# Sums of the last 64 queries on 64x64 tiles, with partial sums in two PSUM banks, and six output buffers

## The chip, the cores and the metric

The kernel runs on one core of one Trainium2 chip. The metric is the device time of one execution in microseconds. The kernel before takes 341.7 us (median of 3 runs, 341.29 to 341.9). TensorE was granted 0.995 to 1.0 of its clock in all runs but those of one experiment, which is marked. A ratio is the mean time of one kernel's fast runs over that of the other's of the same rounds, so it is not quite the ratio of the medians quoted beside it.

## The reference

Attention over 8 batches, 12 heads, 448 positions of 64 dimensions, with one added to the softmax denominator (in its shifted form), followed by a feed-forward layer with a maximum over three products (put together from the reference's two functions):

```python
scores = scale * np.matmul(q, k.transpose(0, 1, 3, 2))
e = np.exp(scores - m)
attn = e / (np.sum(e, axis=-1, keepdims=True) + np.exp(-m) + 1e-09)
x = np.matmul(attn, v)          # then heads side by side: 3584 x 768
h = np.maximum(np.maximum(x @ w1, x @ w2), x @ w3)
out = h @ w_out
```

## The kernel before

The heads are worked in 24 groups of four, two pairs of heads each (`i` is the group, `pr` the pair). Each group takes three visits. In a visit TensorE computes scores of one group, then, in two visits of three, for one pair of the group before the weighted sum over keys (`av`), then pieces of the feed-forward layer that keep it busy. 448 queries are four blocks of 128 columns, of which the last is only half needed. 448 keys are three chunks of 128 and a tail of 64; the tails of both heads share 128 partitions and are summed on 64x64 tiles:

```python
def av_tail(i, ej, pr, ws=(0, 1, 2, 3)):         # (cut)
    for j, w in enumerate(ws):
        for hh in range(2):
            for half in range(2):
                nc.tensor.matmul(out=ps[half * HP : half * HP + HP, hh, j * D1 : (j + 1) * D1], ...)  # 64x64

def av_main(i, ej, pr, ws=(0, 1, 2, 3)):         # (cut)
    for hh in range(2):
        for j, w in enumerate(ws):
            for c, x in enumerate((X1, X3, X2)):
                nc.tensor.matmul(out=ps[:, hh, j * D1 : (j + 1) * D1], lhsT=eF[:, o : o + 128], ...)  # 128x128
    nc.vector.tensor_scalar(out=rb[:, :, 0:nw], in0=acc[:, :, :, D], ... op0=ALU.add)
    nc.vector.reciprocal(out=rb[:, :, 0:nw], in_=rb[:, :, 0:nw])
    nc.vector.tensor_tensor(out=xn[i][...], in0=acc[:, :, :, 0:D], in1=rb..., op=ALU.mult)
```

Column `D` of each sum is the softmax denominator, since the values carry a column of constants. A piece of the feed-forward layer is a group of six matmuls into one of two PSUM buffers, evacuated by VectorE:

```python
ps_b = ctx.enter_context(tc.tile_pool(name="ps_b", bufs=2, space=bass.MemoryType.PSUM))
def up_piece(b, fcs, i, q0, qn):                  # (cut)
    p_i = ps_b.tile([128, 512], FP32, tag="b", name="p_i")
    ...six matmuls...
    if i == 0: nc.vector.tensor_copy(out=dst, in_=src)
    else:      nc.vector.tensor_tensor(out=dst, in0=dst, in1=src, op=ALU.max)
```

`out_piece` does the same for the last product (`op_ps`, evacuated into `o_sb`, then a transfer to `out`).

The softmax here doesn't subtract the row's maximum and nothing guards it: scores larger than these inputs give would overflow.

## Time and profile before

| | kernel before |
|---|---|
| time, median | 341.7 us |
| TensorE (PE) busy | 330.3 us, 97% |
| VectorE (DVE) busy | 188.4 us, 55% |
| chain that ended last | PE 93%, DVE 2% |
| idle of PE just before p_i groups | 1.1 us |

The busy share says who has no room. The chain, followed back from the last instruction, says whose work the end waited for. The timeline says what happens around one sum. The lines are in the prediction.

### The profile page before, as it was taken

Reading aid. Unit: us, or ns where it says so; the run is one execution under the profiler, and the core shown is the slowest. Engines: PE = TensorE matmul, PEld = TensorE weight load, DVE = VectorE, ACT = ScalarE, POOL = GpSimd, SP = SyncE. Lnnn points to the kernel's source line nnn. Section 1 sums busy time; section 2 is a strip of 40 time slices with the busy share of each in tenths; the row PEclk is TensorE's granted clock in tenths of the full one; section 3 lists DMA queues with packets and bytes.
Section 4 is the critical chain, followed back from the end, with each engine's and each line's share of the span. In section 5 each row is a group of like instructions: output and inputs, shape, how many; then the busy total and the mean of one; then the engine's idle time right before and its main releaser. Section 6 shows DMA issues by size and latency. Waiting matters only on the chain.

```text
span 340.8 us, 9819 instructions
## 1 busy us (share of the span) xinstructions
PE 330.3 (97%) x4174; PEld 199.6 (59%) x4174; DVE 188.4 (55%) x410; ACT 151.2 (44%) x181; POOL 146.7 (43%) x260
## 2 busy tenths in 40 slices
PE   7899999999999999999999999999999999999994
PEld 4668787855555645555655655565545655565552
DVE  4556675565545365546456556556556556465552
ACT  3858855654554535463544454463544454200000
POOL 8596578971937072925267070946252000000000
PEclk9999999999999999999999999999999999999999
DMA  8999999699996999999986999999960440133006
GB/s 145 190 191 206 203 205 197 115 170 212 134 164 60 178 213 110 156 138 185 157 119 90 190 199 116 155 127 194 167 115 10 119 123 3 31 78 95 0 19 167
DMA packets 84813, 46.42 MB, mean 136 GB/s; under 512 B 53281, under 2 KB 81313, under 8 KB 84769
## 3 DMA queue, kind: packets, MB, share of 16 engines
q0 software_dynamic: 29120, 21.80, 48.6%
q1 hardware_dynamic: 55264, 23.60, 36.7%
q8 instruction: 32, 0.52, 0.6%
q10 hardware_dynamic: 384, 0.39, 0.4%
q14 instruction: 13, 0.10, 0.1%
HBM read 44.04 MB, written 11.01 MB: 162 GB/s over the span
## 4 chain that ended last, share of the span: by engine, by line
PE 93%; ACT 2%; DVE 2%; issue 1%; ACTq 0%
PE p_i L440 48%; PE op_ps L464 16%; PE avp L357 12%; PE stp L300 12%; PE avp L340 2%; ACT e L320 2%; PE warm L171 1%; PE trT L225 1%; ACT QT L184 1%; DVE QT L186 1%; PE trT L209 1%; DVE xn L373 1%; PE xtp L413 0%; PE xtp L400 0%; DVE xT L406 0%
## 5 line engine op out<-in xcount | busy, mean ns | idle before, releaser
L320 ACT ACTIVATE e<-stp 128x896 f16<-128x896 f32 (+4 forms) x171 | 144.3, 905 | 138.2 <-PE stp L300 138.0
L440 PE MATMUL p_i<-xT,w 128*128 128x448 f16 (+2 forms) x972 | 173.4, 332 | 1.1 <-DVE o_sb L471 0.8
L440 PEld LDWEIGHTS <-w 128*128 128x128 f16 x972 | 90.0, 98 | 69.0 <-issue 6.6
L245 POOL COPY QT<-QT 64x384 f16<-64x384 f16 (+1 forms) x84 | 46.9, 559 | 95.4 <-DMA QT<-ld_q 65.0
L451 DVE TENSOR_TENSOR hT<-hT,p_i 128x448 f16<-128x448 f16 (+2 forms) x96 | 59.7, 621 | 43.0 <-PE p_i L440 42.8
L464 PE MATMUL op_ps<-w,hT 128*128 128x384 f16 (+2 forms) x342 | 58.1, 323 | 0.0
L300 PE MATMUL stp<-QT,KT 64*64 64x448 f16 (+2 forms) x756 | 48.4, 339 | 2.3 <-ACT e L320 0.9
L464 PEld LDWEIGHTS <-hT 128*128 128x128 f16 x342 | 32.1, 98 | 23.0 <-issue 2.0
L471 DVE TENSOR_SCALAR o_sb<-op_ps 128x384 f32<-128x384 f32 (+2 forms) x57 | 31.2, 549 | 25.8 <-PE op_ps L464 22.7
L357 PE MATMUL avp<-vx,e 128*128 128x65 f16 x1152 | 45.4, 193 | 0.0
L449 DVE CAST hT<-p_i 128x448 f16<-128x448 f32 (+2 forms) x48 | 30.0, 625 | 24.3 <-PE p_i L440 24.2
L357 PEld LDWEIGHTS <-e 128*128 128x128 f16 x1152 | 38.8, 97 | 2.3
L373 DVE TENSOR_TENSOR xn<-avp,rb 128x512 f16<-128x512 f32 (+1 forms) x54 | 34.1, 632 | 1.9
L300 PEld LDWEIGHTS <-KT 64*64 64x64 f16 x756 | 16.0, 105 | 27.0 <-issue 24.2
L367 DVE TENSOR_SCALAR rb<-avp 128x8 f32<-128x8 f32 (+1 forms) x54 | 8.9, 165 | 39.4 <-PE avp L357 39.2
L383 POOL COPY vx<-ld_v 128x768 f16<-128x768 f16 x21 | 17.2, 820 | 8.3 <-issue 4.7
L340 PEld LDWEIGHTS <-e 64*64 64x64 f16 x768 | 14.7, 107 | 8.0 <-issue 1.2
L102 POOL DMA_DIRECT2D ld_q<-in_q_dram x24 | 17.2, 718 | 2.1 <-DMA w<-in_moe_w_dram 1.1
L102 POOL DMA_DIRECT2D ld_k<-in_k_dram x24 | 17.2, 718 | 1.9 <-DMA w<-in_moe_w_out_dram 1.0
L115 POOL DMA_DIRECT2D ld_v<-in_v_dram x24 | 15.1, 631 | 2.6 <-DMA w<-in_moe_w_dram 1.4
L340 PE MATMUL avp<-vt,e 64*64 64x65 f16 x768 | 15.4, 192 | 0.5 <-ACT e L320 0.4
L112 POOL DMA_DIRECT2D ld_v<-in_v_dram x24 | 15.2, 633 | 1.2 <-DMA w<-in_moe_w_dram 1.2
(43 smaller groups left out, 88.2 us busy)
## 6 DMA issues: line engine op xcount, KB each, us to landing
out_dram<-o_sb SPq DMA_DIRECT2D x54, 192.0 KB, 3.2
ld_v<-in_v_dram POOLq DMA_DIRECT2D x48, 128.0 KB, 4.8
ld_k<-in_k_dram POOLq DMA_DIRECT2D x23, 224.0 KB, 6.2
ld_q<-in_q_dram POOLq DMA_DIRECT2D x23, 224.0 KB, 7.0
w<-in_moe_w_dram POOLq DMA_DIRECT2D x9, 384.0 KB, 9.5
w<-in_moe_w_out_dram POOLq DMA_DIRECT2D x3, 384.0 KB, 8.5
xT<-xn SPq DMA_TRANSPOSE x18, 4.3
QT<-ld_q SPq DMA_TRANSPOSE x17, 5.1
```

What stands on the lines that cost most here:

```text
L102: nc.gpsimd.dma_start(out=tiles[nm][:, 1 : NP * T + 1].rearrange("x (r t) d -> x r (t d)", r=NP)[:, p0:p1], in_=src[:, p0:p1],)
L245: eng.tensor_copy(out=t[d0 : d0 + HP, o * 128 : (o + n) * 128], in_=t[s0 : s0 + HP, a * 128 : (a + n) * 128],)
L300: nc.tensor.matmul(out=stp[half * HP : half * HP + HP, par, j * qn : (j + 1) * qn], lhsT=k_block(i, pr, h2, x[half]), rhs=q_cols(i, pr, h2 ...
L320: nc.scalar.activation(out=dst, in_=src, func=AF.Exp, scale=scale)
L340: nc.tensor.matmul(out=ps[half * HP : half * HP + HP, hh, j * D1 : (j + 1) * D1], lhsT=eF[hh * HP : hh * HP + HP, o : o + HP], rhs=vt[hh * ...
L357: nc.tensor.matmul(out=ps[:, hh, j * D1 : (j + 1) * D1], lhsT=eF[:, o : o + 128], rhs=vx[:, 2 * pr + hh, (x[0]), 0:D1], start=False, stop= ...
L373: nc.vector.tensor_tensor(out=xn[i][:, pr, ws[0] : ws[0] + nw].rearrange("p j h d -> p h j d"), in0=acc[:, :, :, 0:D], in1=rb[:, :, 0:nw]. ...
L440: nc.tensor.matmul(out=p_i[:, j * qn : (j + 1) * qn], lhsT=w_sb[i][:, dc, ts(fc, 128)], rhs=xT[b][:, dc, q0 : q0 + qn], start=(dc == 0), s ...
L449: nc.vector.tensor_copy(out=dst, in_=src)
L451: nc.vector.tensor_tensor(out=dst, in0=dst, in1=src, op=ALU.max)
L464: nc.tensor.matmul(out=op_ps[:, 0:w], lhsT=hT[bp][:, fc, ts(t, 128)], rhs=wout_sb[:, fc, c : c + w], start=(fc == 0), stop=(fc == NFC - 1),)
L471: nc.vector.tensor_scalar(out=o_sb[:, c : c + w], in0=op_ps[:, 0:w], scalar1=1.0 / LAMBDA, scalar2=None, op0=ALU.mult,)
```

## The change

The last 64 queries of each pair had their sums on full 128x128 matmuls of which half the output columns were thrown away. The change computes them as 64x64 tiles, in sets of four (the 64x64 tail tiles of the kernel before start mostly 3 to 4 ns apart within a set, and the sets 29 to 36 ns apart in nearly all sums): rows of the array are the two halves of the keys, columns the two heads. In the code, two tiles that hold different key halves write two different PSUM banks, so the halves are added on VectorE. It applies from group 6 on, in 36 sums. Two smaller parts come along: the opening is reordered without two dummy matmuls, and the output gets six buffers. The results `xn` move into three fixed buffers, whose part that nothing writes is cleared once (cut below).

```diff
-    out_pool = ctx.enter_context(tc.tile_pool(name="outp", bufs=3))
+    out_pool = ctx.enter_context(tc.tile_pool(name="outp", bufs=6))
+    def av_last(i, ej, pr):                      # (cut) 2 tail tiles and 12 tiles of 64x64
+        for c, x in enumerate((X1, X3, X2)):
+            for r in range(2):
+                for hh in range(2):
+                    tile_mm(r, hh, o, rhs, c == 2)   # out=ps[head hh's half, bank r]
     # av_main, after the denominators of the three full blocks
+        if last:
+            nc.vector.tensor_copy(out=end, in_=ps[:, 1, 3 * D1 : 4 * D1])
+            nc.vector.tensor_tensor(out=end, in0=ps[:, 0, 3 * D1 : 4 * D1], in1=end, op=ALU.add)
+            nc.vector.tensor_scalar(out=rb_all[:, 2 * nw :], in0=end[:, D:], ... op0=ALU.add)
     nc.vector.reciprocal(...); nc.vector.tensor_tensor(... op=ALU.mult)   # now 3 blocks
+        if last:
+            for hh in range(2):                  # head 1 moves from partitions 64.. to 0..
+                nc.vector.tensor_scalar(out=xn[i][0:HP, pr, 3, hh], in0=end[h, 0:D],
+                                        scalar1=rb_all[h, 2 * nw :], op0=ALU.mult)
-    warm(2)
-    attend("O", 2, ("v", 1, 0), ("v", 1, 1), ("v", 2, 0))
+    attend("O", 2, ("v", 1, 0))
     attend("E", 0, S01)
+    attend("O", 2, ("v", 1, 1), ("v", 2, 0), ("v", 2, 1))
```

More of the change, by code (lines that the diff above doesn't have):

```diff
@@ L58 @@
     PE_X = 2
+    LAST = 6
     NEB = 2
@@ L64 @@
     small = ctx.enter_context(tc.tile_pool(name="small", bufs=3))
-    xn_pool = ctx.enter_context(tc.tile_pool(name="xn", bufs=3))
     xt_pool = ctx.enter_context(tc.tile_pool(name="xt", bufs=3))
     ht_pool = ctx.enter_context(tc.tile_pool(name="ht", bufs=2))
-    out_pool = ctx.enter_context(tc.tile_pool(name="outp", bufs=3))
+    out_pool = ctx.enter_context(tc.tile_pool(name="outp", bufs=6))
     ps_s = ctx.enter_context(tc.tile_pool(name="ps_s", bufs=3, space=bass.MemoryType.PSUM))
@@ L166 @@
         nc.vector.memset(blk[:, :, NO : NO + HP], 0.0)
+    xn_buf = [cpool.tile([P, NP, 4, 2, D], MMDT, name=f"xn{j}") for j in range(NV)]
+    for j in range(NV):
+        nc.vector.memset(xn_buf[j][HP:P, :, 3], 0.0)
     def warm(n, cols=512):
@@ L347, in av_tail, with tile_mm, av_main @@
                     )
-    def av_main(i, ej, pr, ws=(0, 1, 2, 3)):
+    def av_last(i, ej, pr):
+        eF, vx, vt = e_buf[ej], v_buf[i % NV], vt_buf[i % NV]
+        ps = avs[i, pr]
+        def tile_mm(r, hh, o, rhs, stop):
+            nc.tensor.matmul(
+                out=ps[hh * HP : hh * HP + HP, r, 3 * D1 : 4 * D1],
+                lhsT=eF[r * HP : r * HP + HP, o : o + HP],
+                rhs=rhs,
+                start=False,
+                stop=stop,
+                skip_group_check=True,
+            )
+        n = where[pr, None, TL]
+        for hh in range(2):
+            tile_mm(hh, hh, e_col(n, 3), vt[hh * HP : hh * HP + HP, pr, 0:D1], False)
+        for c, x in enumerate((X1, X3, X2)):
+            for r in range(2):
+                for hh in range(2):
+                    o = e_col(where[pr, hh, x], 3)
+                    rhs = vx[r * HP : r * HP + HP, 2 * pr + hh, x[0], 0:D1]
+                    tile_mm(r, hh, o, rhs, c == 2)
+    def av_main(i, ej, pr, ws=(0, 1, 2, 3), last=False):
         eF, vx = e_buf[ej], v_buf[i % NV]
@@ L365, in av_main @@
         acc = ps[:, :, 0 : nw * D1].rearrange("p h (j d) -> p h j d", d=D1)
-        rb = small.tile([P, 2, 4], FP32, tag="rb", name="rb")
+        rb_all = small.tile([P, 2 * nw + 1], FP32, tag=f"rb{nw}", name="rb")
+        rb = rb_all[:, 0 : 2 * nw].rearrange("p (h j) -> p h j", h=2)
         nc.vector.tensor_scalar(
-            out=rb[:, :, 0:nw], in0=acc[:, :, :, D], scalar1=1.0 / LAMBDA, scalar2=None, op0=ALU.add
+            out=rb, in0=acc[:, :, :, D], scalar1=1.0 / LAMBDA, scalar2=None, op0=ALU.add
         )
-        nc.vector.reciprocal(out=rb[:, :, 0:nw], in_=rb[:, :, 0:nw])
+        if last:
+            end = small.tile([P, D1], FP32, tag="end", name="end")
+            nc.vector.tensor_copy(out=end, in_=ps[:, 1, 3 * D1 : 4 * D1])
+            nc.vector.tensor_tensor(
+                out=end, in0=ps[:, 0, 3 * D1 : 4 * D1], in1=end, op=ALU.add
+            )
+            nc.vector.tensor_scalar(
+                out=rb_all[:, 2 * nw :], in0=end[:, D:], scalar1=1.0 / LAMBDA, scalar2=None,
+                op0=ALU.add,
+            )
+        rb_in = rb_all if last else rb_all[:, 0 : 2 * nw]
+        nc.vector.reciprocal(out=rb_in, in_=rb_in)
         if i not in xn:
-            xn[i] = xn_pool.tile([P, NP, 4, 2, D], MMDT, tag="xn", name="xn")
+            xn[i] = xn_buf[i % NV]
         nc.vector.tensor_tensor(
@@ L375, in av_main @@
             in0=acc[:, :, :, 0:D],
-            in1=rb[:, :, 0:nw].unsqueeze(3).to_broadcast([P, 2, nw, D]),
+            in1=rb.unsqueeze(3).to_broadcast([P, 2, nw, D]),
             op=ALU.mult,
         )
+        if last:
+            for hh in range(2):
+                h = slice(hh * HP, hh * HP + HP)
+                nc.vector.tensor_scalar(
+                    out=xn[i][0:HP, pr, 3, hh], in0=end[h, 0:D], scalar1=rb_all[h, 2 * nw :],
+                    scalar2=None, op0=ALU.mult,
+                )
     def prep_v(i, eng):
@@ L528, in av @@
     def av(i, ej, pr, part):
-        av_tail(i, ej, pr, PW[part])
-        av_main(i, ej, pr, PW[part])
+        if i >= LAST:
+            av_tail(i, ej, pr, (0, 1, 2))
+            av_last(i, ej, pr)
+            av_main(i, ej, pr, (0, 1, 2), True)
+        else:
+            av_tail(i, ej, pr, PW[part])
+            av_main(i, ej, pr, PW[part])
     load_weight(0)
@@ L568 @@
     x_transpose_pe(0, "O")
-    warm(2)
-    attend("O", 2, ("v", 1, 0), ("v", 1, 1), ("v", 2, 0))
+    attend("O", 2, ("v", 1, 0))
     attend("E", 0, S01)
+    attend("O", 2, ("v", 1, 1), ("v", 2, 0), ("v", 2, 1))
     x_transpose_pe(1, "O")
-    attend("E", 0, ("v", 2, 1), S23)
+    attend("E", 0, S23)
     x_transpose_pe(2, "O")
```

## The prediction

> **What bounds the kernel now.** I read the page first: the busy shares, then the chain that ended last.
>
> ```profile
> PE 330.3 (97%) x4174; PEld 199.6 (59%) x4174; DVE 188.4 (55%) x410; ACT 151.2 (44%) x181; POOL 146.7 (43%) x260
> PE 93%; ACT 2%; DVE 2%; issue 1%; ACTq 0%
> ```
>
> TensorE is busy for 330.3 of 340.8 us and carries 93% of the chain, at full granted clock. So a nanosecond taken from TensorE is a nanosecond of the span, and so is one for which TensorE is made to wait. VectorE is busy 55% of the time, which looks like ample room. Whether it is depends on when VectorE's work falls, so next I read the timeline around one sum (one pair of heads, one `av` call).
>
> ```profile
> 183.12 0.29 PE L340 MATMUL avp<-vt,e 64*64 64x65 f16 x16
> 183.35 0.92 PE L357 MATMUL avp<-vx,e 128*128 128x65 f16 x24
> ...
> 184.12 1.29 PE L440 MATMUL p_i<-xT,w 128*128 128x448 f16 x6
> 184.31 0.17 DVE L367 TENSOR_SCALAR rb<-avp 128x8 f32<-128x8 f32 x1 [0.86 <-PE avp L357]
> 184.51 0.20 DVE L370 RECIPROCAL rb<-rb 128x8 f32<-128x8 f32 x1
> 184.75 0.69 DVE L373 TENSOR_TENSOR xn<-avp,rb 128x512 f16<-128x512 f32 x1
> 185.45 0.62 DVE L451 TENSOR_TENSOR hT<-hT,p_i 128x448 f16<-128x448 f16 x1
> ```
>
> The sum takes 16 matmuls on 64x64 tiles (the key tails), then 24 full ones; TensorE goes straight on to the next group of the feed-forward part (p_i, six matmuls, 1.135 us from group to group). VectorE begins to normalise 0.19 us after that group's start, needs three instructions that end 1.13 us later, and is then just in time to evacuate the first group. The groups rotate through two PSUM buffers, so the third group after a sum can't start before the first is evacuated. That makes VectorE's 1.13 us a quantity with a limit.
>
> The same view elsewhere shows the limit being hit once, by another cause:
>
> ```profile
> 119.11 1.02 DVE L471 TENSOR_SCALAR o_sb<-op_ps 128x384 f32<-128x384 f32 x2 [2.92 <-PE avp L357]
> 119.72 0.54 PE L440 MATMUL p_i<-xT,w 128*128 128x448 f16 x2 [0.76 <-DVE o_sb L471]
> ```
>
> VectorE stood for 2.92 us. The releaser named had ended earlier; the instruction order shows that this eviction also waits for the output transfers that free one of three output buffers. TensorE restarted 0.05 us after the first eviction ended (119.11 + 0.555 = 119.67), having lost 0.76 us. So a late eviction does stop TensorE.
>
> [...] single records have the last four tail matmuls at 183.217 us and the first full one at 183.349, 132 ns against some 31 within a mode. The change puts its small matmuls between tails and full ones, so it adds no switch. [...] (3 to 4 ns within a set of four; the next four follow 29 to 33 ns later). [...] a copy from partition 64 started 0.03 us after the previous copy's end, where unheld independent instructions start some 0.08 us before it.
>
> **The change on TensorE.** It applies from group 6 on: 18 groups by 2 pairs, 36 sums. Each loses six full matmuls of 31.8 ns ((184.117 - 183.353) / 24): -191 ns. In place of tail matmuls in four sets of four there are three sets of tails, and for the last queries four more rounds on the busiest tiles: seven rounds for four, at 31 ns: +93 ns. Net about -97 ns, times 36 = **-3.5 us**. Six output buffers remove the one stall: **-0.8 us**. At the start, the two dummy matmuls go and the first scores of group 0's other queries come earlier; the sum there then waits for ScalarE instead, so of the 0.43 us little is won, but the waits of 0.37 us for xn and some 0.4 us for xT near 22.7 and 23.4 us shrink in part: **-0.3 us**, an estimate. Together -4.6 us.
>
> **The change on VectorE.** These rows size the new instructions (groups by line, shapes apart; the last two numbers before the bar's idle time are busy us and mean ns):
>
> ```profile
> L449 DVE CAST hT<-p_i 128x448 f16<-128x448 f32 x42 | 26.2, 625 | 20.6 <-PE p_i L440 20.6
> L373 DVE TENSOR_TENSOR xn<-avp,rb 128x512 f16<-128x512 f32 x42 | 29.0, 692 | 1.4
> L373 DVE TENSOR_TENSOR xn<-avp,rb 128x256 f16<-128x256 f32 x12 | 5.1, 425 | 0.4
> L370 DVE RECIPROCAL rb<-rb 128x8 f32<-128x8 f32 x42 | 8.5, 203 | 1.4
> L370 DVE RECIPROCAL rb<-rb 128x4 f32<-128x4 f32 x12 | 2.1, 179 | 0.4
> L186 DVE CAST ld_k<-first_k 128x448 f16<-128x448 f32 x1 | 0.4, 396 | 2.0 <-DMA first_k<-in_k_dram 2.0
> ```
>
> From L373, (692 - 425) / 256 = 1.04 ns an element and 158 ns fixed from PSUM. [...] Hence: sums' column of 6: 164 ns (167 for 8, 161 for 4); copy of 128x65: 226; add of 128x65: 226; the 128x1 addition: about 150; reciprocal of 7: 197; product of 128x384: 558; two products of 64x64: about 190 each (least certain). Dependent instructions follow after 34 ns, independent ones overlap by 80 ns. Laid out from the first one's start: 0; copy 0.084 to 0.310; add 0.344 to 0.570; addition 0.604 to 0.754; reciprocal 0.788 to 0.985; product 1.02 to 1.58; first small product 1.50 to 1.69; second, held, 1.72 to 1.91. The next eviction starts at 1.83 if it reads only PSUM, or 1.94 if it also reads hT [...]. Today it could start at 1.05. So the sequence grows by some 0.8 us; 36 of these are about 28 us of VectorE time, which by itself would cost nothing.
>
> **What the longer sequence costs.** Count from the first group's start after a sum. For p_i groups the third can start at 2.27 us. Its buffer is free at 0.19 + 1.83 (or 1.94) + 0.62 of eviction + 0.05 = 2.69 (2.80): a stall of 0.42 or 0.53. For op_ps groups (0.975 us each, eviction 0.556): 0.19 + 1.83 + 0.556 + 0.05 = 2.63 against 1.95: 0.67. If only two groups follow before the next scores, the pause of scores and sums hides it.
> From the TensorE timeline I counted what follows each of the 36 sums: 14 times three p_i groups (first eviction a cast 7 times, a maximum 7 times), 5 times three op_ps groups, once a p_i and two op_ps groups; the last two sums are back to back; 14 are followed by two groups only. Stalls: 14 x 0.475 = 6.65; 5 x 0.67 = 3.35; 2.80 - 2.11 = 0.69; and for the last pair, whose sequences queue on VectorE, 1.35. Sum **+12.0 us**. Today the same sum gives no stall (0.19 + 1.14 + 0.62 + 0.05 = 2.00 < 2.27), and the page agrees: all idle of TensorE before p_i groups is 1.1 us.
>
> Result: 341.7 - 4.6 + 12.0 = **349 us**, +2.1%.
>
> **Rivals.** (a) The stalls don't come, because VectorE's small instructions take nearer 60 to 100 ns than 150 to 190: the next eviction starts near 1.55, the stalls shrink to some 5.5 us and the total is about 342.5. For it speaks that VectorE is idle 45%, and memsets take as little as 62 ns; against it, that every record reading data takes at least 151 ns. (b) Stalls are short or absent and the TensorE saving shows in full: 337 us. Against it speaks the two-buffer count above. (c) The small matmuls don't overlap as the tails do, say because each waits for its weights: then the saving is nearly nil, and the total 352. Against it speaks the measured 31 ns a round, weight loads included. (d) POOL's copies in SBUF slow VectorE's new SBUF instructions: copies of 64x128 vary from 168 to some 276 ns today; 0.1 us more a sum adds 2 us.
>
> **Range and chances.** Each 0.1 us in VectorE's sequence moves 21 stalls, so 2.1 us. I take 0.15 us either way for that, and 1.5 us for TensorE's part: 344 to 353. The middle lies just above the 2% line (348.5), so slower and within are nearly even; faster by 2% needs both no stall and a larger saving than TensorE has: 0.02.
>
> **What would show it.** Right: TensorE idle before p_i and op_ps groups, waiting for VectorE, grows from 1.1 to some 12 us, in pieces of 0.4 to 0.7 us at the third group after a sum; full sum matmuls go from 1152 to 936; the wait of 2.92 us is gone. Wrong: that idle stays below 4 us, or the next eviction follows the first normalising instruction by under 1.5 us, or the small matmuls take more than 31 ns for four.

The sum keeps all its terms: 341.7 - 4.6 + 12.0 = 349.1, given as 349. The 190 ns of the two products stand as estimate alone: they came from the 396 ns of the one ld_k record and a rate from SBUF that no run shows. The eviction at 1.83 or 1.94 us, and so the +12.0 us, hang on them. The 0.11 us between these two starts are put together from the copies from partition 64 (three records, which started 31 to 32 ns after the end of the copy before) and the 80 ns by which independent instructions overlap; that a maximum would be held like those copies was an estimate too (after the change a cast starts at 1.91 and a maximum at 2.02 us). The numbers in brackets, 3 to 4 ns and 29 to 33, are of the starts of the tail matmuls.

## The result, and the profile after

The changed kernel takes **357.84 us** (357.08 to 358.18, 4 runs) against 341.54 us: ratio 1.0473, 95% interval 1.0453 to 1.0494. It is slower by 16.3 us, more than twice the 7.3 us that were predicted, and outside the range of 344 to 353 us. The page of the changed kernel, its busy shares and its chain:

```profile
PE 330.4 (93%) x4316; PEld 196.4 (55%) x4316; DVE 218.9 (62%) x593; ACT 151.0 (43%) x181; POOL 146.5 (41%) x260
PE 73%; DVE 20%; issue 3%; ACT 2%; ACTq 0%; DVEq 0%
```

VectorE's part of the chain went from 2% to 20%, though it is busy only 62% of the time. TensorE's busy time did not fall although its work did. That is an effect of the record: a p_i matmul is shown for about 350 ns where the next one normally starts after 189, so each stop adds some 0.16 us of shown busy time.

The timeline around one sum that op_ps groups follow (start in us, duration in us, engine, line, operation, count, idle time before it and what ended it):

```profile
198.26 2.11 PE L514 MATMUL op_ps<-w,hT 128*128 128x384 f16 x12
198.46 0.17 DVE L399 TENSOR_SCALAR rb<-avp 128x6 f32<-128x6 f32 x1 [0.83 <-PE avp L388]
198.54 0.21 DVE L404 COPY end<-avp 128x65 f32<-128x65 f32 x1
198.79 0.23 DVE L405 TENSOR_TENSOR end<-avp,end 128x65 f32<-128x65 f32 x1
199.05 0.15 DVE L408 TENSOR_SCALAR rb<-end 128x1 f32<-128x1 f32 x1
199.24 0.20 DVE L413 RECIPROCAL rb<-rb 128x7 f32<-128x7 f32 x1
...
199.47 0.56 DVE L416 TENSOR_TENSOR xn<-avp,rb 128x384 f16<-128x384 f32 x1
199.95 0.51 DVE L425 TENSOR_SCALAR xn<-end,rb 64x64 f16<-64x64 f32 x2
200.37 1.02 DVE L521 TENSOR_SCALAR o_sb<-op_ps 128x384 f32<-128x384 f32 x2
...
200.98 1.14 PE L514 MATMUL op_ps<-w,hT 128*128 128x384 f16 x6 [0.60 <-DVE o_sb L521]
```

Two groups (12 matmuls) fill the two buffers. The third stands still until VectorE has worked through eight instructions and evacuated the first. The eviction starts 1.91 us after the first normalising instruction (1.05 before).

Where POOL copies in SBUF at the same time, it is worse. Here the two products take 1.16 us together, and TensorE stands for 1.12:

```profile
184.54 2.38 POOL L249 COPY QT<-QT 64x384 f16<-64x384 f16 x4 [2.59 <-DMA QT<-ld_q]
184.60 1.16 DVE L425 TENSOR_SCALAR xn<-end,rb 64x64 f16<-64x64 f32 x2
...
185.79 0.62 DVE L501 TENSOR_TENSOR hT<-hT,p_i 128x448 f16<-128x448 f16 x1
...
186.46 1.29 PE L490 MATMUL p_i<-xT,w 128*128 128x448 f16 x6 [1.12 <-DVE hT L501]
```

And one kind of stop comes already in the second group. The op_ps group needs hT, which the eviction of the p_i group before it writes; its sixth matmul waits for that:

```profile
190.12 0.98 PE L514 MATMUL op_ps<-w,hT 128*128 128x384 f16 x5
...
191.32 0.62 DVE L501 TENSOR_TENSOR hT<-hT,p_i 128x448 f16<-128x448 f16 x1
...
192.00 0.34 PE L514 MATMUL op_ps<-w,hT 128*128 128x384 f16 x1 [0.90 <-DVE hT L501]
```

The groups by line, shapes apart (busy us, mean ns after the bar), give the sizes of VectorE's new instructions:

```profile
L425 DVE TENSOR_SCALAR xn<-end,rb 64x64 f16<-64x64 f32 x72 | 22.2, 308 | 0.5
L416 DVE TENSOR_TENSOR xn<-avp,rb 128x384 f16<-128x384 f32 x36 | 20.1, 557 | 1.4 <-DVE rb L413 0.2
L405 DVE TENSOR_TENSOR end<-avp,end 128x65 f32<-128x65 f32 x36 | 8.2, 227 | 1.2
L404 DVE COPY end<-avp 128x65 f32<-128x65 f32 x36 | 7.8, 217 | 0.0
L413 DVE RECIPROCAL rb<-rb 128x7 f32<-128x7 f32 x36 | 7.2, 201 | 1.2
L399 DVE TENSOR_SCALAR rb<-avp 128x6 f32<-128x6 f32 x36 | 5.9, 164 | 23.8 <-PE avp L388 23.8
L408 DVE TENSOR_SCALAR rb<-end 128x1 f32<-128x1 f32 x36 | 5.5, 154 | 1.2
```

All are within 9 ns of the prediction but the products, of mean 308 ns instead of 190. Instruction by instruction, where no POOL record overlaps them, the first takes 237 and the second 252 ns; the longest take 527 and 654.

I added up how much later than its normal pitch each feed-forward matmul starts after the 36 sums. Before: 0.3 us. After: **18.4 us**, behind 23 sums. The loss is smaller because TensorE saves some 4 us elsewhere; 1 to 2 us of the loss are not in these delays (below).

### The profile page after: what moved, and what is told of

Same layout as the page of the kernel before. It is cut to its first block, busy times and chain, and to the rows that moved or that the text cites. A ratio compares the mean times of both kernels' runs of the same rounds, so it can differ in the third digit from the quotient of the medians.

```text
span 355.3 us, 10283 instructions
## 1 busy us (share of the span) xinstructions
PE 330.4 (93%) x4316; PEld 196.4 (55%) x4316; DVE 218.9 (62%) x593; ACT 151.0 (43%) x181; POOL 146.5 (41%) x260
## 4 chain that ended last, share of the span: by engine, by line
PE 73%; DVE 20%; issue 3%; ACT 2%; ACTq 0%; DVEq 0%
PE p_i L490 35%; PE op_ps L514 13%; PE stp L304 11%; PE avp L388 9%; DVE xn L425 4%; DVE xn L416 4%; DVE hT L501 2%; DVE rb L413 2%; ACT e L324 2%; DVE end L405 2%; PE avp L344 1%; DVE rb L399 1%; PE warm L175 1%; PE avp L361 1%; DVE rb L408 1%
## 5 line engine op out<-in xcount | busy, mean ns | idle before, releaser
L490 PE MATMUL p_i<-xT,w 128*128 128x448 f16 (+2 forms) x972 | 175.6, 332 | 7.7 <-DVE hT L501 4.2
L514 PE MATMUL op_ps<-w,hT 128*128 128x384 f16 (+2 forms) x342 | 59.1, 323 | 7.5 <-DVE hT L501 4.3
L388 PE MATMUL avp<-vx,e 128*128 128x65 f16 x936 | 38.6, 194 | 0.0
L388 PEld LDWEIGHTS <-e 128*128 128x128 f16 x936 | 32.0, 97 | 2.3
L416 DVE TENSOR_TENSOR xn<-avp,rb 128x384 f16<-128x384 f32 (+2 forms) x54 | 29.3, 543 | 2.1 <-DVE rb L413 0.2
L399 DVE TENSOR_SCALAR rb<-avp 128x6 f32<-128x6 f32 (+2 forms) x54 | 8.8, 164 | 33.5 <-PE avp L388 33.5
L425 DVE TENSOR_SCALAR xn<-end,rb 64x64 f16<-64x64 f32 x72 | 22.2, 308 | 0.5
L344 PEld LDWEIGHTS <-e 64*64 64x64 f16 x624 | 13.7, 107 | 7.9 <-issue 1.4
```

The source lines that it names most:

```text
L416: nc.vector.tensor_tensor(out=xn[i][:, pr, ws[0] : ws[0] + nw].rearrange("p j h d -> p h j d"), in0=acc[:, :, :, 0:D], in1=rb.unsqueeze(3) ...
L425: nc.vector.tensor_scalar(out=xn[i][0:HP, pr, 3, hh], in0=end[h, 0:D], scalar1=rb_all[h, 2 * nw :], scalar2=None, op0=ALU.mult,)
L490: nc.tensor.matmul(out=p_i[:, j * qn : (j + 1) * qn], lhsT=w_sb[i][:, dc, ts(fc, 128)], rhs=xT[b][:, dc, q0 : q0 + qn], start=(dc == 0), s ...
L514: nc.tensor.matmul(out=op_ps[:, 0:w], lhsT=hT[bp][:, fc, ts(t, 128)], rhs=wout_sb[:, fc, c : c + w], start=(fc == 0), stop=(fc == NFC - 1),)
```

## The experiments

The theory: the loss is made by the length of VectorE's sequence between a sum and the first eviction behind it. Rivals: TensorE's small matmuls cost time themselves; one of the two side parts does harm; POOL's copies lengthen the new instructions; the amount of VectorE work counts and not its place.

**One part at a time.** Four kernels, all starting from the kernel before. The first takes only the opening:

```diff
-    warm(2)
-    attend("O", 2, ("v", 1, 0), ("v", 1, 1), ("v", 2, 0))
+    attend("O", 2, ("v", 1, 0))
     attend("E", 0, S01)
+    attend("O", 2, ("v", 1, 1), ("v", 2, 0), ("v", 2, 1))
```

> The kernel before with only the new order of the opening (no two dummy matmuls, first scores of group 0's other queries earlier). If the loss comes from VectorE's longer sequence after each sum: about 341.3 us, 0.2 us below the kernel before. Rival, the new opening upsets the later rhythm: well above 345 us.

Measured: 341.12 against 341.85 us, ratio 0.9979 (0.9966 to 0.9993). A gain of 0.7 us, no harm.

The second takes only the output buffers:

```diff
-    out_pool = ctx.enter_context(tc.tile_pool(name="outp", bufs=3))
+    out_pool = ctx.enter_context(tc.tile_pool(name="outp", bufs=6))
```

> The kernel before with only six output buffers. Expected: the 2.92 us wait of VectorE and the 0.76 us stop of TensorE go, 340.8 us. Rival, the stop is only moved elsewhere: 341.5 us, unchanged. In either case no loss.

Measured: 341.49 against 341.85 us, ratio 0.9989 (0.9976 to 1.0002). The wait and the stop are gone from the trace. The gain, 0.4 us, is not clear of noise; no harm either.

The third takes only TensorE's side of the new sums:

```diff
+            av_tail(i, ej, pr, (0, 1, 2)); av_last(i, ej, pr); av_main(i, ej, pr, (0, 1, 2), True)
     # av_main: no copy, addition, inverse or products for the last 64 queries (left zero, wrong on purpose)
```

> The kernel before with the 64x64 matmuls for the last 64 queries, but none of the new VectorE instructions (those results are left out, so the output is wrong on purpose). If TensorE's new matmuls save what the count of rounds says: 36 times 0.1 us, 338.0 us, with no new stalls of TensorE. Rival, the small matmuls or the larger number of instructions cost TensorE time themselves: 345 us or more.

Measured: 338.8 against 341.85 us, ratio 0.9913 (0.9899 to 0.9927). The small matmuls save 3.0 us. Its page:

```profile
PE 326.3 (97%) x4318; PEld 195.6 (58%) x4318; DVE 183.9 (55%) x413; ACT 151.0 (45%) x181; POOL 146.6 (44%) x260
```

TensorE's busy time falls by 4 us here, where no stops hide the saving. The first rival falls.

The fourth takes only VectorE's side, with the full matmuls kept:

```diff
+            nc.vector.tensor_copy(out=end, in_=ps[:, 1, 3 * D1 : 4 * D1])
+            nc.vector.tensor_tensor(out=end, in0=ps[:, 0, 3 * D1 : 4 * D1], in1=end, op=ALU.add)
+            nc.vector.tensor_scalar(out=r1, in0=end[:, D:], ... op0=ALU.add)
         nc.vector.reciprocal(...); nc.vector.tensor_tensor(...)      # as before
+            for hh in range(2): nc.vector.tensor_scalar(out=scr[:, hh], in0=end[h, 0:D], scalar1=r1[h], ...)
```

> The kernel before with its matmuls unchanged, plus five VectorE instructions of the changed kernel's kinds and shapes in each of the 36 sums (results to a scratch tile; the output stays right). If the longer sequence alone makes the loss: stalls of 18 us as in the changed kernel, and some 2.5 us more because the large product keeps its 128x512 (0.134 us in each of about 21 stalls): about 361 us. Rival, the loss needs the new matmuls: about 342 us.

Measured: 361.06 against 341.85 us, ratio 1.0563 (1.0548 to 1.0577), with correct output. Its page, busy shares and chain:

```profile
PE 333.6 (93%) x4174; PEld 199.6 (56%) x4174; DVE 221.9 (62%) x590; ACT 151.1 (42%) x181; POOL 146.9 (41%) x260
PE 70%; DVE 20%; issue 3%; DMA 3%; ACT 2%; POOL 1%; POOLq 0%; ACTq 0%; DVEq 0%
```

Five VectorE instructions a sum, which nobody needs, cost 19.2 us; the delays of feed-forward matmuls in its trace add to 19.4 us. The 2.5 us more that I had expected from the larger product did not come: where POOL is not in the way the first eviction starts at 1.92 or 2.04 us, hardly later than in the changed kernel, since the reciprocal here does not wait for the 128x1 addition (it starts at 201.72 us, the addition ends at 201.80). So the loss is VectorE's, and the new matmuls are not needed for it.

**The new sums without the side parts.** The changed kernel with the old opening and three output buffers:

```diff
-    out_pool = ctx.enter_context(tc.tile_pool(name="outp", bufs=6))
+    out_pool = ctx.enter_context(tc.tile_pool(name="outp", bufs=3))
     # and the four lines of the opening as in the kernel before
```

> The changed kernel with three output buffers and the old opening, so the new sums alone. If VectorE's sequence makes the loss and the other two parts are worth 0.4 and 0.7 us as their own runs showed: 358.5 to 359.5 us. Rival, the parts interact: outside 357 to 361.

Measured: 359.41 against 341.57 us, ratio 1.0513 (1.0484 to 1.0542). The parts add up as expected; its runs spread more (357.98 to 360.6).

**Are the long products POOL's doing?** The added halves go back to PSUM, so that the products read PSUM:

```diff
-            nc.vector.tensor_tensor(out=end, in0=ps[:, 0, 3 * D1 : 4 * D1], in1=end, op=ALU.add)
+            end = ps[:, 0, 3 * D1 : 4 * D1]
+            nc.vector.tensor_tensor(out=end, in0=end, in1=half1, op=ALU.add)
```

> The changed kernel, but the added halves go back to PSUM, so that the two small products read PSUM instead of SBUF. If the products' long instances (up to 652 ns) come from POOL copying in SBUF at the same time: both products keep about 225 to 260 ns whether POOL copies or not, the stalls fall from 18.4 to about 16 us, total 355 to 356 us. Rival, they are long for another reason: still instances over 350 ns, total near 357.8.

Measured: 358.63 against 341.57 us, ratio 1.0497 (1.0482 to 1.0512). The group of the products, by line:

```profile
L424 DVE TENSOR_SCALAR xn<-avp,rb 64x64 f16<-64x64 f32 x72 | 20.1, 279 | 0.5
```

Single records lie between 266 and 269 ns for the first product and 289 and 290 for the second, whether POOL copies or not; in the changed kernel they reached 654. So POOL's copies lengthen the products, in these traces, only when they read SBUF. The time did not fall, a miss: the undisturbed products are 30 to 40 ns longer from PSUM, and in every sum but the last two the eviction now starts at 2.17 us (first pair of a group) or 2.10 us (second pair), whether it is a cast or a maximum, instead of at 1.91 in the best. The delays add to 20.5 us.

**Place or amount: the products later.** The two products move behind the first eviction; the work is the same:

```diff
-            for hh in range(2):
-                nc.vector.tensor_scalar(out=xn[i][0:HP, pr, 3, hh], ...)
+            late.append(products)
     # fill(): after each feed-forward piece
             f(*a)
+            if late:
+                late.pop(0)()
-                x_transpose_dma(i - 1)       # reads the products
+                late.append(lambda b=i - 1: x_transpose_dma(b))
```

> The changed kernel with only the two small products moved on VectorE behind the eviction of the first feed-forward group after the sum (same work, other order). If the place in VectorE's order and not its amount makes the loss: the first eviction starts 1.49 us after the first normalising instruction instead of 1.91 to 2.68, the stalls fall to about 5 us, total about 344 us. Rival, the amount of VectorE work counts: about 357 us.

Measured: 343.78 against 341.57 us, ratio 1.0069 (1.0052 to 1.0085). From 357.84 us, moving two instructions, and the issue of the transfer that reads their result, took 14 us off. The delays that remain add to 5.9 us, where about 5 were expected. The timeline of one sum:

```profile
196.55 3.28 PE L494 MATMUL p_i<-xT,w 128*128 128x448 f16 x16
...
197.57 2.38 POOL L249 COPY QT<-QT 64x384 f16<-64x384 f16 x4 [6.84 <-DMA QT<-ld_q]
197.77 0.56 DVE L417 TENSOR_TENSOR xn<-avp,rb 128x384 f16<-128x384 f32 x1
198.24 0.61 DVE L503 CAST hT<-p_i 128x448 f16<-128x448 f32 x1
198.77 1.22 DVE L427 TENSOR_SCALAR xn<-end,rb 64x64 f16<-64x64 f32 x2
```

POOL copies here too, and the products take 1.22 us, but the first eviction is already done. VectorE is busy 218.7 us, as in the changed kernel (218.9). So the place counts and not the amount.

The kernels together give a straight line. For three p_i groups after a sum, the time from the first normalising instruction to the first eviction, and the delay of the third group (sums without POOL in the way):

| kernel | to first eviction, us | third group late by, us |
|---|---|---|
| before | 1.13 | 0 |
| products later | 1.49 | 0.09 |
| changed, eviction a cast | 1.91 | 0.51 |
| changed, eviction a maximum | 2.02 | 0.63 |
| products from PSUM, second pair of a group | 2.10 | 0.71 |
| products from PSUM, first pair of a group | 2.17 | 0.78 |

The delay is the first column less 1.40 us: two groups take 2.27 us, of which 0.20 pass before the first normalising instruction, 0.62 go to the eviction and 0.05 to the restart.

**All of the late work later.** Three steps behind three evictions:

```diff
+            late.extend([add_halves, inverse, products])
-                x_transpose_dma(i - 1)
+                late.append(lambda b=i - 1: x_transpose_dma(b))
```

> The changed kernel with all VectorE work for the last 64 queries moved behind the evictions, in three steps: the added halves behind the first, the inverse behind the second, the products behind the third. Same instructions and one reciprocal more. If only the place counts: no stalls beyond the kernel before, TensorE's saving shows, about 337 to 338 us, faster than both kernels. Rival, the amount counts: about 357 us or more.

Measured: 351.13 us median, but from 341.99 to 354.15, with a granted clock of 0.982 to 0.988 in the four runs above 350, which are classed slow. The two fast runs, 345.77 and 341.99 us, are no faster than the kernel before. The profiled run is a slow one, so I use it only to find where the new wait is:

```profile
PE p_i L499 <- DMA xT<-xn: 11.9, 4, 7.9
```

Behind a sum the late work itself no longer stops TensorE, except behind the last two sums. But my edit had also put the transposing transfer of xn behind the third step. For the longest wait, 7.9 us, it was issued at 150.16 us, where the products-later kernel issues it at 146.84, and it landed 13.2 us later (median of that run 6.0). Why it took so long I did not find out. In this trace the lower clock comes behind the waits: `--windows` gives 1.00 from 100 to 154.8 us, before the wait, and 0.50 from 163.3 to 166, behind it, where p_i matmuls start 373 ns apart instead of 189; behind the other long wait, of 2.8 us, it is 0.59 from 244.5 to 247. The three other slow runs left no trace. The expectation was missed by my own edit: whatever is held back holds back its readers too.

**The same in two steps,** halves behind the first eviction, inverse and products behind the second, the transfer at the end of the same visit at the latest:

```diff
-            late.extend([add_halves, inverse, products])
+            late.extend([add_halves, inverse_products])
             fill(per)
+            flush()
```

> As late_all, but in two steps (halves added behind the first eviction; inverse and products behind the second), and the transposing transfer of xn is issued at the end of the same visit at the latest. If late_all lost its time only because that transfer was issued too late (7.9 us wait for xT): no such wait, no stalls at the third group, 337 to 338 us, ahead of both kernels. Rival, VectorE's amount of work still costs: above 341 us.

Measured: 340.14 against 341.64 us, ratio 0.9948 (0.9914 to 0.9983). The long waits are gone. It is 0.5% faster than the kernel before, and so faster than the changed one, but by less than expected: 0.65 us went once to a late xT, and 0.9 us to delays behind the last two sums. Its yardstick is the kernel before with both side parts:

```diff
-    out_pool = ctx.enter_context(tc.tile_pool(name="outp", bufs=3))
+    out_pool = ctx.enter_context(tc.tile_pool(name="outp", bufs=6))
     # and the opening of the changed kernel
```

> The kernel before with the two small parts only, new opening and six output buffers. If they add up: 0.7 + 0.4 us, about 340.6 us. The reference for what the new sums themselves are worth in late_two_steps.

Measured: 340.88 against 341.64 us, ratio 0.9967 (0.993 to 1.0005); as expected, though the interval touches 1. One of the nine runs of the kernel before that were taken beside these two, 344.71 us, lies 3 us above the others; without it the ratios of the means are 0.996 for the two steps and 0.998 here.

**The last group left as it was,** so that no late work queues up behind the last two sums:

```diff
-        if i >= LAST:
+        if LAST <= i < NI - 1:
```

> late_two_steps with the last group (its two sums stand back to back and its xT is needed soon) left on the old full matmuls. If the 0.94 us of waits at the end come from VectorE's queue there: they go, 0.2 us of TensorE saving is given up, about 339.4 us. Rival, they are part of the end in any case: 340.1 us or more.

Measured: **339.38** against 341.61 us, ratio 0.9922 (0.9893 to 0.9952), the best of the kernels with correct output (0.993 without one run of the kernel before at 344.56 us). Of its 2.2 us some 0.8 belong to the side parts, so about 1.5 us are left for the new sums, of the 3.0 that TensorE's side saved alone. By the core's span it is 3.1 us ahead, since its runs have 2.1 to 2.8 us outside the span and the kernel before 1.8; why, I did not look. Its page, and its timeline around one sum:

```profile
PE 326.8 (97%) x4308; PEld 196.0 (58%) x4308; DVE 226.7 (67%) x617; ACT 151.0 (45%) x181; POOL 146.4 (43%) x260
```

```profile
193.94 3.57 PE L503 MATMUL p_i<-xT,w 128*128 128x448 f16 x18
194.14 0.17 DVE L400 TENSOR_SCALAR rb<-avp 128x6 f32<-128x6 f32 x1 [0.54 <-PE avp L389]
194.34 0.19 DVE L404 RECIPROCAL rb<-rb 128x6 f32<-128x6 f32 x1
194.56 0.56 DVE L407 TENSOR_TENSOR xn<-avp,rb 128x384 f16<-128x384 f32 x1
...
195.27 0.62 DVE L512 CAST hT<-p_i 128x448 f16<-128x448 f32 x1 [0.15 <-PE p_i L503]
195.81 0.22 DVE L418 COPY end<-avp 128x65 f32<-128x65 f32 x1
196.06 0.23 DVE L419 TENSOR_TENSOR end<-avp,end 128x65 f32<-128x65 f32 x1
196.41 0.62 DVE L514 TENSOR_TENSOR hT<-hT,p_i 128x448 f16<-128x448 f16 x1
```

All 18 matmuls of three groups run without a stop. VectorE is even idle for 0.15 us before the first eviction. It is busier than in the changed kernel (226.7 us against 218.9), and the kernel is 18 us faster.

**All in one step** behind the first eviction, to issue the transfer earlier:

```diff
-            late.extend([add_halves, inverse_products])
+            late.append(rest)          # add_halves(); inverse_products()
```

> As late_two_steps_x, but all of the late VectorE work in one step behind the first eviction, so that the transposing transfer of xn is issued about 0.7 us earlier. If the late transfer is what still costs: about 339 us. Rival, the block of some 1.3 us behind the first eviction delays the second one: stalls at the next group again, 341 us or more.

Measured: 340.76 against 341.61 us, ratio 0.9962 (0.9932 to 0.9992). Between the two expectations: the delays behind the sums stay at 0.3 us as in the kernel before, yet the median is 1.4 us above the two steps. The runs of the two kernels touch (338.66 to 339.73, and 339.52 to 341.35). The spans differ as well, by 1.6 us in the mean. What costs the difference I did not settle.

Not tested: more than two PSUM buffers for the feed-forward groups, and evictions on another engine than VectorE.

## Why the prediction was wrong

**The mechanism was right.** VectorE idle for 45% of the time did not protect TensorE, since what counts is how soon after a sum the first eviction comes. Most of the waits came where they were counted, at the third group, behind VectorE; those of three sums came in the second group. Rival (a) falls, since the small instructions took 154 to 227 ns; (b) falls by the 18.4 us of delays, (c) by the 3.0 us that the small matmuls save; (d), POOL's copies, is real: 1.9 us, where 2 were put, but that they agree is luck, since it came as up to 0.65 us in 6 sums and not as 0.1 us in each.

**TensorE's part held.** Predicted -4.6 us in three terms: -3.5, -0.8, -0.3. By ratios to the kernel before: -3.0 (small matmuls), -0.4 (buffers, not clear of noise), -0.7 (opening). Sum -4.1.

**The step that failed is "What the longer sequence costs": +12.0 us, measured 18.4.** Two of its terms were mis-sized and one overlap in it was wrong, with about equal weight:

1. "Two products of 64x64: about 190 each (least certain)". Undisturbed they take 237 and 252 ns. The estimate rested on a single record, the 396 ns of ld_k, and on a rate from SBUF that no run shows. That puts the eviction at 1.91 and 2.02 us instead of 1.83 and 1.94, and each of the 19 plain stops is 0.1 us longer, that behind the last pair 0.17: 2.0 us. (14 x 0.571 + 5 x 0.765 + 1.52 = 13.3 against 6.65 + 3.35 + 1.35 = 11.35.)
2. POOL was put among the rivals and not into the sum, and read too small there: the 276 ns of rival (d) are a mean of three, and the single copies of 64x128 on VectorE took 173 to 440 ns. Its copies, and in one case its issuing of transfers, met the products in 6 of the sums that stop TensorE and added 1.9 us there (the largest: 1.285 us of delay for 0.63). One eviction of an op_ps group came 0.2 us later without POOL: the product of the full blocks before it started 0.23 us after the reciprocal instead of 0.03, and the trace does not show what held it. Together 2.1 us.
3. "If only two groups follow before the next scores, the pause of scores and sums hides it." Not where the first is a p_i and the second an op_ps group: the sixth matmul of the second reads what the eviction of the first writes. Two of the 14 sums that I had counted as free stopped TensorE for 0.96 us each, and the one sum followed by a p_i and two op_ps groups stopped there too, for 0.96 instead of 0.69: 2.2 us. I had counted only the PSUM buffers and missed this dependency, which the code shows: here the overlap was wrong, not a size.

2.0 + 2.1 + 2.2 = 6.3, of 18.4 - 12.0 = 6.4 us. (One more reading is slightly off, without effect on the sum: the first full matmul behind the tails starts at 183.353 us, so the switch takes 136 ns from start to start and not 132.)

Put together for the profiled run (357.08 us): 341.5 - 4.1 + 18.4 = 355.8. The 1.3 us left are partly one stop of 0.33 us before an op_ps group behind scores, which my sum over the 36 sums does not hold; about 1 us I can't assign. The other runs were up to 1.1 us slower.

The range was too narrow on the slow side. A sum of some 20 equal waits multiplies an error in one instruction by 20, and I gave "0.15 us either way" for terms of which I had called one least certain and had left another at zero.

## What to carry to other kernels

When the bounding engine writes to two rotating buffers, the engine that empties them has a deadline, and its idle share says nothing of it: add up its instructions between the trigger and the first eviction, and compare with two groups' time (here 0.20 + 1.91 + 0.62 + 0.05 us against 2.27: the third group was late by 0.51). What is not needed at once belongs behind the evictions, in pieces that fit between them, together with the early issue of whatever reads it (two products moved: 343.78 us instead of 357.84). Follow the data that an eviction writes as well as the buffer that it frees (three stops of 0.96 us here).
